# Parking half of the first MLP's input weights in the P tiles, moving their spills in the program, and loading queries first

## The chip, the cores and the metric

One core of one Trainium2 chip runs the whole kernel. The metric is the device time of one execution in microseconds (us). Each run below was taken on the same kind of core; a profile is one execution recorded by the hardware profiler.

## The reference

A Nystrom attention over 4 batches and 8 heads of 576 tokens (head size 64, 32 landmarks) is followed by two MLPs over the 2304 tokens (512 to 2048 to 512). Cut to what matters:

```python
q_lm = q.reshape(B, H, 32, 18, 64).mean(axis=3)      # landmarks of queries, and of keys alike
A, Bm, C = sm(q, k_lm), sm(q_lm, k_lm), sm(q_lm, k)  # sm: scaled scores, softmax over the last axis
Z = Bm.T / (norm1(Bm) * norminf(Bm) + 1e-6)
for _ in range(6):
    Z = 2 * Z - Z @ Bm @ Z
x = A @ Z @ C @ v                                    # then heads side by side: 2304 x 512
h = x @ w_in;  y = (h - tanh(h)) @ w_out             # first MLP
h = y @ w_in2; out = (h * tanh(softplus(h))) @ w_out2
```

## The kernel before

**Weights.** The four weight matrices come as 64-bit numbers. Each 128x512 piece (512 KB) is loaded into a *raw* buffer by the queue of SyncE (SP, line 123; there are four raw buffers). ScalarE (ACT) then makes the upper part of each float32 from it (`f32_a`, L136, called **the cast** below, into one of two *top* tiles), and VectorE (DVE) joins the lower bits to it (`f32_b`, L140, called **the join**), which frees the raw buffer. The generator `convert` runs down a list of 32 such pieces for the first MLP: 4 pieces of the input weights `w1i` (part j = 0), 9 of the output weights `w1o`, the other 12 of `w1i` (parts 1 to 3), and 7 more of `w1o`. They are numbered #1 to #32 below, in this order. It fetches three pieces ahead.

**Input weights of the first MLP.** They are folded into the attention: for each batch b and part j, `p_gen(b, j)` multiplies the little matrix `Z0` with them into a tile P (128 x 2 x 2 x 512 in float32). Batch 0 is computed in one float32 pass and uses only the first half P[:, :, 0, :]; the other batches use both halves (high and low parts). All batches need the weights, so the joined tiles of batch 0 (name `w1`, four buffers for eight tiles of 512 KB) are written out to DRAM (`w1s`, **the spill**, eight of them, issued by GpSimd's queue, POOL, in `keep_job`, L295) and read back for the later batches (`w1_load`, L617).

**Slots.** After a prologue (batch 0's attention up to `Z0`, and the first 16 casts), the first MLP runs in 128 slots, 32 per batch. Slot s multiplies one 128-wide block of P with the attention (`h1(s)`, L656 in batch 0), ACT and DVE work out h - tanh(h) (`vec(s)`: L682 s, L683 th, L685 q, L698 q on ACT; L688 mk, L694 g, L695 th, L705 g, L709 g on DVE), and `y1(s - 3)` multiplies with `w1o` (L726 in the first 16 slots). The `h` tiles have two buffers, so `h1(s)` waits for the last reader of `h1(s - 2)`, which is L695. Beside the slots run the conversion (two pieces a slot in slots 0 to 3, then one), and the attention of the next batch: its q, k and v are loaded in slot 3 (`attn_load`, L365, and `v_load`, L374 and L375), its means are DVE's L384.

**Order.** Each engine runs its instructions in the order in which a scheduler wrote them when the kernel was built; an instruction waits on its engine's queue for semaphores, and what stands behind it waits too. A DMA belongs to the queue of the engine that issues it.

Of the kernel before, what the change touches and what calls it, by code (L numbers as in the profile page):

```python
# [29 lines left out]
def kernel(  # L30
# [97 lines left out]

    tops = [const.tile([128, 512, 2], F16, name=f"top{i}") for i in range(2)]

    last_P, last_h = [None], [None]

    def f32_a(raw, i):
        top = tops[i % 2]
        with tc.issue_after(last_P[0]) if last_P[0] else ExitStack():
            A.activation(out=top[:, :, 1], in_=raw.bitcast(BF16)[:, :, 2], func=ACTF.Copy)  # L136
        return raw.bitcast(U32)[:, :, 0], top.bitcast(U32)[:, :, 0]

    def f32_b(low, top, t):
        V.scalar_tensor_tensor(out=t.bitcast(U32), in0=low, scalar=13, in1=top,  # L140
                               op0=ALU.logical_shift_right, op1=ALU.bitwise_or)
        yield 0


# [140 lines left out]
        yield 1  # L285

    def keep_job(src, g, j, a):
        def where():
            if a == 0:
                w1t[0, g, j] = w1_p.tile([128, 2, 512], F32, tag="w1", name="w1")  # L290
            return w1t[0, g, j][:, a, :]

        def done(y):
            if a == 1:
                G.dma_start(out=w1s[g, j], in_=w1t[0, g, j])  # L295
                if g:
                    ready.append(j)
        return src, done, where

    def convert(jobs, ahead=3):  # L300
        n = len(jobs)
        raws, st, halves = {}, {}, {}

        def fetch(i):
            if i < n:
                raws[i] = load_raw(jobs[i][0])

        for i in range(ahead):
            fetch(i)
# [11 lines left out]
    ready = []  # L321
    w1t = {}


# [23 lines left out]
    def heads(o, lhs, rhs):  # L348

        for c in range(4):  # L350
            ps = slice(32 * c, 32 * c + 32)
            mm(o[ps], lhs[ps], rhs[ps], start=True, stop=True, tile_position=(32 * c, 32 * c))

    ATt = {}
    adone = set()
# [3 lines left out]
    def attn_load(b, g):  # L359
        r = inp[b, g] = {}  # L360
        r["q"] = in_p.tile([128, 2, S], F32, tag="q", name="q")
        r["k"] = in_p.tile([128, 2, S + M], F32, tag="k", name="k")
        for t, src in ((r["k"], kT), (r["q"], qT)):
            if b:
                nc.sync.dma_start(out=t[:, :, 0:S], in_=src[b, 2 * g:2 * g + 2].rearrange("a p s -> p a s"))  # L365
            else:
                for a in range(2):
                    nc.sync.dma_start(out=t[:, a, 0:S], in_=src[b, 2 * g + a])
# [8 lines left out]
    def attn_pre(b):  # L377
# [17 lines left out]
            A.activation(out=(KB, QB)[x][:, g:4:2, :], in_=red[:, g, x], func=ACTF.Copy, scale=1.0 / R)  # L395

        todo = []
        for g in range(NG):
            for x, t in enumerate((ks[g], qs[g])):
                yield 1  # L400
                if todo:
                    scaled(*todo.pop())
                mean(g, x, t)
                todo.append((g, x))
                yield 1
        yield 1
        scaled(*todo.pop())
        yield 1
# [4 lines left out]
        for hf in range(2):  # L413
            for g in range(NG):
                inp[b, g]["c"] = c[:, g]
            if b == 0 and hf:
                pp = [ps_y.tile([128, 512], F32, tag="y", name="y") for g in range(NG)]
            else:
                pp = [ps_m.tile([128, 512], F32, tag="m", name="m") for g in range(NG)]
            blocks([p[:, 0:NH] for p in pp], QB, lambda ps, g, a: ks[g][ps, a, NH * hf:NH * hf + NH],  # L420
                   b > 0)
            yield 1
            n = NH - M * hf
            for g, p in enumerate(pp):
                A.activation(out=c[:, g, NH * hf:NH * hf + NH], in_=p[:, 0:NH], func=ACTF.Copy)
                V.tensor_reduce(out=mx[:, g, hf:hf + 1], in_=p[:, 0:n], axis=AX.X, op=ALU.max)
                yield 0
                if hf:
                    V.tensor_reduce(out=mx[:, g, 3:4], in_=p[:, n:NH], axis=AX.X, op=ALU.max)
                    yield 0  # L430
            yield 1
# [4 lines left out]
        V.tensor_scalar(out=nb, in0=mx[:, :, 2:4], scalar1=-0.125, scalar2=None, op0=ALU.mult)  # L436
        su = sm_p.tile([128, NG, 2], F32, tag="su", name="su", bufs=1)
        for g in range(NG):
            A.activation(out=c[:, g, S:S + M], in_=c[:, g, S:S + M], func=ACTF.Exp, bias=nb[:, g, 1:2],
                         scale=0.125, accum_out=su[:, g, 1:2])  # L440
        for g in range(NG):
            A.activation(out=c[:, g, 0:S], in_=c[:, g, 0:S], func=ACTF.Exp, bias=nb[:, g, 0:1],
                         scale=0.125, accum_out=su[:, g, 0:1])
        yield 1
        yield 1
        yield 1
# [49 lines left out]

        py = ps_m.tile([128, 512], F32, tag="m", name="m")
        for g in range(NG):
            heads(py[:, 32 * g:32 * g + 32], bb[:, 1, g, :], bb[:, 1, g, :])
        yield 1  # L500
        pv = ps_m.tile([128, 512], F32, tag="m", name="m")
        for g in range(NG):
            for j in range(5):
                n = 128 if j < 4 else 64
                for i in range(4):
                    c4 = slice(32 * i, 32 * i + 32)
                    h = 2 * (i // 2) + g
# [98 lines left out]
        adone.add((b, g, hf))  # L606
        yield 1

    Pt = {}
    done = set()  # L610

    def w1_load(n):
# [5 lines left out]

    def p_gen(b, j):
        ws = [w1t.pop((b, g, j)) for g in range(NG)]  # L620
        P = Pt[b, j] = P_p.tile([128, NG, 2, 512], F32R if b else F32, tag="P", name="P")
        pp = [ps_m.tile([128, 512], F32, tag="m", name="m") for g in range(NG)]
        blocks(pp, Z0, lambda ps, g, a: ws[g][ps, a, :])
        n = 2 * (4 * b + j) + 2
        if b or j == 3:
            w1_load(n)
            w1_load(n + 1)
        yield 1
        for g, p in list(enumerate(pp))[::1 if b else -1]:
# [382 lines left out]
    if True:  # L1012
        for g in range(NG):
            attn_load(0, g)
        setup()

        def w1i_jobs(j):
# [15 lines left out]
        while live or nc_ < PREP:  # L1033
            st = []
            if "pre" in live:
                st.append("pre")
            if n >= 15 and "pa" in live:
                st.append("pa")
            if n == 1:
                for g in range(NG):  # L1040
                    v_load(0, g)
            gens = []
            for k in st:
                if part(live[k]):
# [12 lines left out]
            n += 1  # L1057
# [103 lines left out]
```

## Time and profile before

| | |
|---|---|
| median of 3 runs | 834.3 us (833.07 to 834.39) |
| the profiled execution | 833.09 us, its span in the trace 831.3 us |
| busy: PE, DVE, ACT, POOL | 786.5, 591.7, 510.0, 207.5 us |
| DMA | 123.62 MB, busy 9 tenths or more in the first slices of the span |
| the chain that ended last | PE 62%, DVE 13%, ACT 10%, DMA 5% |

PE is TensorE's matmuls, POOL is GpSimd. A busy PE is modelled, so a stretch of 100% means that matmuls were queued without a gap. A wait in brackets behind an instruction is the idle time of its engine just before it and what ended it. Lines L... are those of the kernel before.

### The profile page before, as it was taken

What the parts mean: (1) busy time and instruction counts of PE and PEld (TensorE: products, weight loads), DVE (VectorE), ACT (ScalarE), POOL (GpSimd) and SP (SyncE); (2) the same over time, 40 slices, a digit from 0 to 9 for tenths busy, and PEclk for the clock granted to TensorE, in tenths of its full rate; (3) what the DMA queues carried; (4) which work ended last, traced back from release to release, by engine and by line L of the source; (5) the groups of instructions that cost most, each with busy time, mean ns of one, the idle gap of its engine ahead of it and who ended that gap; (6) DMA issues with size and microseconds to landing.
All of it is one profiled execution on the core that took longest, in us unless ns stands there. A gap on an engine that the chain in (4) does not pass through costs nothing.

```text
span 831.3 us, 14769 instructions
## 1 busy us (share of the span) xinstructions
PE 786.5 (95%) x5384; PEld 671.5 (81%) x5384; DVE 591.7 (71%) x1300; ACT 510.0 (61%) x1213; POOL 207.5 (25%) x233
## 2 busy tenths in 40 slices
PE   4788999999999999999998999999999999999996
PEld 1345688789987999788887888888889888888885
DVE  7679999998799877999898788786433356334332
ACT  5477877888777977787887566656223236323222
POOL 0010006786687756864340000000000000000000
PEclk9999999999999999999999999999999999999999
DMA  9899341421224100331407756864525523523402
GB/s 327 320 321 364 124 143 41 150 100 53 93 71 168 52 31 2 112 109 38 130 18 277 268 227 240 300 232 147 196 88 167 172 93 140 203 88 104 163 1 76
DMA packets 41512, 123.62 MB, mean 149 GB/s; under 512 B 5856, under 2 KB 14560, under 8 KB 38368
## 3 DMA queue, kind: packets, MB, share of 16 engines
q1 hardware_dynamic: 40288, 118.49, 40.7%
q0 software_dynamic: 1152, 4.19, 1.2%
q8 instruction: 42, 0.69, 0.3%
q14 instruction: 30, 0.25, 0.1%
HBM read 94.36 MB, written 28.31 MB: 148 GB/s over the span
## 4 chain that ended last, share of the span: by engine, by line
PE 62%; DVE 13%; ACT 10%; DMA 5%; issue 5%; POOL 5%; SPq 0%; ACTq 0%; DVEq 0%; POOLq 0%
PE h L821 6%; PE h L819 6%; PE h L820 5%; PE y L731 4%; PE y L879 4%; PE y L878 4%; PE y L877 4%; PE y L735 4%; PE y L732 4%; PE h L656 3%; PE m L334 2%; PE m L878 2%; PE m L879 2%; PE m L877 2%; DVE g L709 2%
## 5 line engine op out<-in xcount | busy, mean ns | idle before, releaser
L832 ACT ACTIVATE gg<-x 128x384 fp32r<-128x384 f32 x72 | 37.8, 525 | 167.0 <-DVE x L842 167.0
L103 POOL TENSOR_TENSOR gg<-g,gg 128x288 fp32r<-128x288 f32 x103 | 97.1, 943 | 160.7 <-ACT gg L102 158.6
L731 PE MATMUL y<-gg,w 128*128 128x288 f32 x448 | 133.9, 313 | 1.7 <-ACT raw L740 1.4
L732 PE MATMUL y<-gg,w 128*128 128x288 f32 x448 | 125.2, 295 | 0.0
L731 PEld LDWEIGHTS y<-gg,w 128*128 128x128 f32 x448 | 84.2, 188 | 21.8 <-issue 12.8
L821 PE MATMUL h<-yk,P 128*128 128x384 f32 x288 | 97.5, 339 | 3.9 <-DVE P L188 3.9
L819 PE MATMUL h<-yk,P 128*128 128x384 f32 x288 | 97.5, 338 | 2.5 <-DVE th L695 1.1
L735 PE MATMUL y<-gg,w 128*128 128x288 f32 x448 | 96.7, 297 | 2.5 <-POOL gg L103 2.5
L820 PE MATMUL h<-yk,P 128*128 128x384 f32 x288 | 96.7, 336 | 0.0
L835 DVE TENSOR_TENSOR gg<-x,gg 128x384 fp32r<-128x384 f32 x72 | 40.2, 558 | 65.9 <-ACT x L833 65.2
L732 PEld LDWEIGHTS y<-gg,w 128*128 128x128 f32 x448 | 84.4, 188 | 0.8
L688 POOL TENSOR_SCALAR mk<-s 128x288 uint8<-128x288 f32 x80 | 78.6, 982 | 10.5 <-ACT s L682 4.2
L842 DVE TENSOR_TENSOR x<-x,h 128x384 f32<-128x384 f32 x72 | 39.8, 552 | 57.8 <-PE h L821 57.8
L709 DVE COPY_PREDICATED g<-mk,th 128x288 f32<-128x288 uint8 x128 | 72.4, 566 | 5.6 <-POOL mk L688 1.7
L879 PE MATMUL y<-w,gg 128*128 128x512 f32 x192 | 75.9, 395 | 0.0
L878 PE MATMUL y<-w,gg 128*128 128x512 f32 x192 | 75.8, 395 | 0.0
L877 PE MATMUL y<-w,gg 128*128 128x512 f32 x192 | 75.3, 392 | 0.0
L735 PEld LDWEIGHTS y<-gg,w 128*128 128x128 f32 x448 | 71.3, 188 | 4.3 <-POOL gg L103 3.5
L694 DVE TENSOR_TENSOR g<-h,s 128x288 f32<-128x288 f32 x128 | 56.9, 444 | 19.4 <-ACT th L683 18.9
L698 ACT ACTIVATE q<-q,bias_c 128x288 f32<-128x288 f32 x128 | 68.6, 536 | 2.6
L682 ACT ACTIVATE s<-h 128x288 f32<-128x288 f32 x128 | 51.9, 406 | 25.2 <-PE h L660 14.9
L102 ACT ACTIVATE gg<-g 128x288 fp32r<-128x288 f32 x112 | 49.5, 442 | 23.8 <-PE y L735 11.2
(170 smaller groups left out, 1889.9 us busy)
## 6 DMA issues: line engine op xcount, KB each, us to landing
P<-w2s SPq DMA_DIRECT2D x16, 1024.0 KB, 4.8
w<-w1s SPq DMA_DIRECT2D x24, 512.0 KB, 4.5
P<-w2s SPq DMA_DIRECT2D x16, 768.0 KB, 5.8
w2s<-P SPq DMA_DIRECT2D x8, 1024.0 KB, 3.9
raw<-in_w1i_dram SPq DMA_DIRECT2D x16, 511.8 KB, 5.9
raw<-in_w1o_dram SPq DMA_DIRECT2D x16, 511.8 KB, 7.0
raw<-in_w2i_dram SPq DMA_DIRECT2D x16, 511.8 KB, 6.3
raw<-in_w2o_dram SPq DMA_DIRECT2D x16, 511.8 KB, 6.4
```

What stands on the lines that cost most here:

```text
L103: eng.tensor_tensor(out=L, in0=src, in1=f32(H), op=ALU.subtract)
L688: eng.tensor_scalar(out=mk, in0=e, scalar1=FT, scalar2=None, op0=ALU.is_ge)
L709: V.copy_predicated(out=g0, mask=mk0, data=t0)
L731: mm(yps[d], w[:, 0, c], gg[:, 0, :], start=(f == 0), stop=False)
L732: mm(yps[d], w[:, 1, c], gg[:, 0, :], start=False, stop=False)
L735: mm(yps[d], w[:, 0, c], gg[:, 1, :], start=False, stop=(f == NF - 1))
L819: mm(t, w[:, i, 0, c], y[a][:, 0], start=(a == 0), stop=False)
L820: mm(t, w[:, i, 0, c], y[a][:, 1], start=False, stop=False)
L821: mm(t, w[:, i, 1, c], y[a][:, 0], start=False, stop=(a == 1))
L877: mm(q, gg[:, 0, cs], w[:, 0, :], start=first, stop=False)
L878: mm(q, gg[:, 0, cs], w[:, 1, :], start=False, stop=False)
L879: mm(q, gg[:, 1, cs], w[:, 0, :], start=False, stop=last)
```

## The change

- `keep_job` no longer takes a `w1` buffer for the second tile of each part (g = 1): it allocates the P tile of batch 0 early and puts the weights in the half that batch 0 leaves empty, P[:, :, 1, :]. `w1` keeps the four tiles of g = 0, and none of its buffers is used twice in batch 0.
- The spills go into a list; the slot loop issues one per slot from slot 11 on (`SPILL`), on the same POOL queue. The first two `w1_load`s of batch 1 move from `p_gen(0, 3)` to slot 21.
- Batch 0's queries are loaded ahead of its keys, and its means are taken in that order. Three raw pieces, and not four, are fetched ahead of v.
- A cast is put behind batch 0's score copies and later behind its softmax exponentials on ACT (`last_act`), a join behind the score maxima on DVE (`last_mx`).
- v of batch 1 is loaded in slot 10 instead of slot 3.
- The matmuls with v (L508) are put behind those of L352.

```diff
     def f32_a(raw, i):
         top = tops[i % 2]
-        with tc.issue_after(last_P[0]) if last_P[0] else ExitStack():
+        with tc.issue_after(last_act[0]):
...
     def f32_b(low, top, t):
-        V.scalar_tensor_tensor(out=t.bitcast(U32), in0=low, scalar=13, in1=top,
-                               op0=ALU.logical_shift_right, op1=ALU.bitwise_or)
+        with tc.issue_after(last_mx[0]):
+            V.scalar_tensor_tensor(out=t.bitcast(U32), in0=low, scalar=13, in1=top,
+                                   op0=ALU.logical_shift_right, op1=ALU.bitwise_or)
...
         def where():
-            if a == 0:
+            if a == 0 and g:
+                Pt[0, j] = P_p.tile([128, NG, 2, 512], F32, tag="P", name="P")
+                w1t[0, g, j] = Pt[0, j][:, :, 1, :]
+            elif a == 0:
                 w1t[0, g, j] = w1_p.tile([128, 2, 512], F32, tag="w1", name="w1")
             return w1t[0, g, j][:, a, :]
 
         def done(y):
             if a == 1:
-                G.dma_start(out=w1s[g, j], in_=w1t[0, g, j])
+                spills.append((w1s[g, j], w1t[0, g, j]))
...
-        for g in range(NG):
-            for x, t in enumerate((ks[g], qs[g])):
-                yield 1
...
+        for g, x in ((0, 0), (0, 1), (1, 0), (1, 1)) if b else ((0, 1), (1, 1), (0, 0), (1, 0)):
+            yield 1
...
-        if b or j == 3:
+        if b:
             w1_load(n)
             w1_load(n + 1)
...
+        for x, src in (("q", qT), ("k", kT)):
+            for g in range(NG):
+                for a in range(2):
+                    nc.sync.dma_start(out=inp[0, g][x][:, a, 0:S], in_=src[0, 2 * g + a])
         setup()
...
-        cv = vec_only(convert(jobs), rate)
+        cv = vec_only(convert(jobs, {i: load_raw(jobs[i][0]) for i in range(3)}), rate)
...
-            if (nc_ < 2 + NPRE or (nc_ < PREP and "pre" not in live)):
+            if last_act[0] and (nc_ < 2 + NPRE or (nc_ < PREP and "pre" not in live)):
...
+                if i >= SPILL and spills:
+                    to, at = spills.pop(0)
+                    G.dma_start(out=to, in_=at)
+                if i == SPILL + 10:
+                    w1_load(8)
+                    w1_load(9)
...
+                    gens["a"] = attn_all(b + 1)
+                if i == (3 if b else 10):
                     for g in range(NG):
                         v_load(b + 1, g)
-                    gens["a"] = attn_all(b + 1)
```

**The order of instructions.** First place: POOL's queue from its setup to the first slot in which it computes (slot 24). Before, with the semaphores that each row waits for (DVE_49 counts DVE's instructions; w_179 and the like are `w1` tiles):

```order
L295 DMA w1s<-w_179 128x1024 [waits DVE_49]
L295 DMA w1s<-w_195 128x1024 [waits DVE_49]
L295 DMA w1s<-w_499 128x1024 [waits DVE_49]
L295 DMA w1s<-w_531 128x1024 [waits DVE_49]
L295 DMA w1s<-w_560 128x1024 [waits DVE_49]
L103 TENSOR_TENSOR gg<-g,gg 128x288 [waits DVE_49,Activation_49]
```

Of the change (the spills are L1085 there):

```order
masks.py:199 AFFINE_SELECT ident<-ident 128x128 [waits Pool_49]
L1085 DMA w1s<-w_227 128x1024 [waits DVE_49]
L1085 DMA w1s<-P 256x1x512 [waits DVE_49]
L1085 DMA w1s<-w_496 128x1024 [waits DVE_49]
L1085 DMA w1s<-w_646 128x1024 [waits DVE_49]
L104 TENSOR_TENSOR gg<-g,gg 128x288 [waits DVE_49,Activation_49]
```

In both there are eight spills in a row with nothing of POOL's between them and the setup; four of the change read P in rows of 512 numbers (2 KB) where `w1` gives rows of 1024 (4 KB). In the built program of the change the counts that they wait for are those of the joins that fill their tiles.

Second place: SP's queue from the last `w1i` piece on. Before:

```order
L123 DMA raw<-in_w1i_dram 128x2047 x12
L365 DMA k<-in_kT_dram 128x2x576
L365 DMA q<-in_qT_dram 128x2x576
L374 DMA v<-in_v_dram 128x4x256
L375 DMA v<-in_v_dram 64x256
L123 DMA raw<-in_w1o_dram 128x2047 x5
L617 DMA w_792<-w1s 128x1024
```

Of the change:

```order
L124 DMA raw<-in_w1i_dram 128x2047 x12
L370 DMA k<-in_kT_dram 128x2x576
L370 DMA q<-in_qT_dram 128x2x576
L124 DMA raw<-in_w1o_dram 128x2047 x7
L376 DMA v<-in_v_dram 128x4x256
L377 DMA v<-in_v_dram 64x256
L622 DMA w_1344<-w1s 128x1024
```

The seven `w1o` pieces #26 to #32 now stand ahead of v (k and q each come twice, v too; the second pairs are left out here).

Third place: ACT and DVE in slots 7 and 8, where the casts and joins of #26 to #28 stand (names top_127 and top_128). ACT before:

```order
L698 ACTIVATE q<-q,bias_c 128x288
L682 ACTIVATE s<-h 128x288
L395 ACTIVATE qb<-red 128x2x32
L685 ACTIVATE q<-s 128x288
L683 ACTIVATE th<-h 128x288
L393 ACTIVATE k<-red 128x2x32
L136 ACTIVATE top_128<-raw 128x512
```

ACT of the change, from the same row:

```order
L705 ACTIVATE q<-q,bias_c 128x288
L137 ACTIVATE top_128<-raw 128x512
L397 ACTIVATE qb<-red 128x2x32
L689 ACTIVATE s<-h 128x288
L690 ACTIVATE th<-h 128x288
L692 ACTIVATE q<-s 128x288
L137 ACTIVATE top_127<-raw 128x512
```

DVE before (the rows from slot 7's mk on):

```order
L688 TENSOR_SCALAR mk<-s 128x288
L694 TENSOR_TENSOR g<-h,s 128x288
L695 TENSOR_TENSOR th<-h,th 128x288
L705 TENSOR_TENSOR g<-q,g 128x288
L384 TENSOR_REDUCE red<-k 128x64
L709 COPY_PREDICATED g<-mk,th 128x288
```

DVE of the change, from the same row:

```order
L695 TENSOR_SCALAR mk<-s 128x288
L142 SCALAR_TENSOR_TENSOR w<-raw,top_128 128x512
L701 TENSOR_TENSOR g<-h,s 128x288
L702 TENSOR_TENSOR th<-h,th 128x288
L712 TENSOR_TENSOR g<-q,g 128x288
L142 SCALAR_TENSOR_TENSOR w<-raw,top_127 128x512
L716 COPY_PREDICATED g<-mk,th 128x288
L386 TENSOR_REDUCE red<-k 128x64
```

The cast and the join of #26 stand some ten rows earlier on ACT's and DVE's queues than before; those of #27 to #30 are spread over slots 7 to 10. The sequences of ACT, DVE and PE up to the join of #25 are the same in both from the start of slot 0 on; behind slot 14 a few rows of DVE and POOL trade places.

## Rows read from the trace of the kernel before

**Rows 1.** Windows: us, then busy us of each engine, PE clock, DMA share, GB/s.
```profile
60.20:85.30 25.10, 22.07 (x107) 14.41 (x105) 21.91 (x49) 18.03 (x46) 0.53 (x1) 0.93 1.02 365
85.30:130.00 44.70, 44.70 (x401) 34.11 (x400) 41.64 (x120) 36.41 (x96) 2.04 (x2) 1.00 0.32 108
```
**Rows 2.** Timeline of POOL: start us, us, instruction, idle before and its releaser.
```profile
44.29 0.53 POOL L295 DMA_DIRECT2D w1s<-w  x1 [24.25 <-DVE w L140]
...
65.48 0.53 POOL L295 DMA_DIRECT2D w1s<-w  x1 [5.59 <-DVE mk L688]
```
**Rows 3.** Timeline of SP's queue.
```profile
57.97 2.30 SPq L374 DMA_DIRECT2D v<-in_v_dram  x1
```
**Rows 4.** The second q of batch 1: duration ns, start us; issue to landing.
```profile
L365 SPq DMA_DIRECT2D q<-in_qT_dram x1: 550/550/550, 57.4 to 57.4; - x1
...
DMA to landing us min/median/max: 13.2/13.2/13.2
```
**Rows 5.** The last spill, the same way.
```profile
L295 POOL DMA_DIRECT2D w1s<-w x1: 533/533/533, 65.5 to 65.5; - x1
...
DMA to landing us min/median/max: 6.7/6.7/6.7
```
**Rows 6.** Chain of waits, 65.71: piece #26 from issue to landing.
```profile
65.71 11.10 DMA raw<-in_w1o_dram
```
**Rows 7.** Piece #29, the same way as rows 4.
```profile
L123 SPq DMA_DIRECT2D raw<-in_w1o_dram x1: 332/332/332, 70.6 to 70.6; - x1
...
DMA to landing us min/median/max: 10.0/10.0/10.0
```
**Rows 8.** Piece #4, and v right behind it, the same way.
```profile
L123 SPq DMA_DIRECT2D raw<-in_w1i_dram x1: 328/328/328, 6.9 to 6.9; - x1
...
DMA to landing us min/median/max: 8.1/8.1/8.1
...
L374 SPq DMA_DIRECT2D v<-in_v_dram x1: 379/379/379, 7.6 to 7.6; - x1
...
DMA to landing us min/median/max: 9.1/9.1/9.1
```
**Rows 9.** Timeline of ACT in slot 7 and later, columns as rows 2.
```profile
71.22 0.54 ACT L698 ACTIVATE q<-q,bias_c 128x288 f32<-128x288 f32 x1
```
**Rows 10.** Timeline of DVE, columns as rows 2.
```profile
61.34 0.69 DVE L140 SCALAR_TENSOR_TENSOR w<-raw,top 128x512 uint32<-128x512 uint32 x1 [1.19 <-ACT top L136]
...
71.00 0.30 DVE L688 TENSOR_SCALAR mk<-s 128x288 uint8<-128x288 f32 x1
...
72.31 1.34 DVE L384 TENSOR_REDUCE red<-k 128x64 f32<-128x1152 f32 x1
73.58 0.47 DVE L709 COPY_PREDICATED g<-mk,th 128x288 f32<-128x288 uint8 x1
...
77.66 0.69 DVE L140 SCALAR_TENSOR_TENSOR w<-raw,top 128x512 uint32<-128x512 uint32 x1 [1.06 <-ACT top L136]
...
80.89 0.69 DVE L140 SCALAR_TENSOR_TENSOR w<-raw,top 128x512 uint32<-128x512 uint32 x1 [0.69 <-ACT top L136]
81.50 0.45 DVE L705 TENSOR_TENSOR g<-q,g 128x288 f32<-128x288 f32 x1
...
84.97 0.45 DVE L695 TENSOR_TENSOR th<-h,th 128x288 f32<-128x288 f32 x1
```
**Rows 11.** Timeline of PE, slots 11 and 12, columns as rows 2.
```profile
82.37 1.24 PE L656 MATMUL h<-AT,P 128*128 128x288 f32 x4
...
85.48 0.75 PE L656 MATMUL h<-AT,P 128*128 128x288 f32 x2
```
**Rows 12.** Timeline of DVE in the prologue, columns as rows 2.
```profile
30.00 0.69 DVE L140 SCALAR_TENSOR_TENSOR w<-raw,top 128x512 uint32<-128x512 uint32 x1 [0.29 <-ACT top L136]
30.70 0.35 DVE L533 SCALAR_TENSOR_TENSOR yv<-yv,m 128x192 f32<-128x192 f32 x1
```
**Rows 13.** Chain of waits, 23.86: piece #9 from issue to landing.
```profile
23.86 5.25 DMA raw<-in_w1o_dram
```

More of the change, by code (lines that the diff above doesn't have):

```diff
@@ L53 @@
     PREP = 16
+    SPILL = 11
     NW = 16
@@ L298, in keep_job, with convert @@
         return src, done, where
-    def convert(jobs, ahead=3):
+    def convert(jobs, raws, ahead=3):
         n = len(jobs)
-        raws, st, halves = {}, {}, {}
+        st, halves = {}, {}
         def fetch(i):
@@ L306, in fetch @@
                 raws[i] = load_raw(jobs[i][0])
-        for i in range(ahead):
-            fetch(i)
         for i in range(n + 2):
@@ L319, in convert @@
             yield 1
-    ready = []
+    Pt = {}
+    ready, spills = [], []
     w1t = {}
@@ L351, in heads @@
             ps = slice(32 * c, 32 * c + 32)
-            mm(o[ps], lhs[ps], rhs[ps], start=True, stop=True, tile_position=(32 * c, 32 * c))
+            last = mm(o[ps], lhs[ps], rhs[ps], start=True, stop=True, tile_position=(32 * c, 32 * c))
+        return last.ins
     ATt = {}
@@ L362, in attn_load @@
         r["k"] = in_p.tile([128, 2, S + M], F32, tag="k", name="k")
[L363 to L368, printed above, removed]
+        for t, src in ((r["k"], kT), (r["q"], qT)) if b else ():
+            nc.sync.dma_start(out=t[:, :, 0:S], in_=src[b, 2 * g:2 * g + 2].rearrange("a p s -> p a s"))
     def v_load(b, g):
@@ L397, in attn_pre @@
         todo = []
-        for g in range(NG):
-            for x, t in enumerate((ks[g], qs[g])):
-                yield 1
[L401 to L405, printed above, removed]
+        for g, x in ((0, 0), (0, 1), (1, 0), (1, 1)) if b else ((0, 1), (1, 1), (0, 0), (1, 0)):
+            yield 1
+            if todo:
+                scaled(*todo.pop())
+            mean(g, x, (ks, qs)[x][g])
+            todo.append((g, x))
+            yield 1
         yield 1
@@ L424, in attn_pre @@
             for g, p in enumerate(pp):
-                A.activation(out=c[:, g, NH * hf:NH * hf + NH], in_=p[:, 0:NH], func=ACTF.Copy)
+                copied = A.activation(out=c[:, g, NH * hf:NH * hf + NH], in_=p[:, 0:NH], func=ACTF.Copy)
                 V.tensor_reduce(out=mx[:, g, hf:hf + 1], in_=p[:, 0:n], axis=AX.X, op=ALU.max)
@@ L430, in attn_pre @@
                     yield 0
+            if b == 0:
+                last_act[0] = hf and copied.ins
             yield 1
@@ L435, in attn_pre @@
         nb = sm_p.tile([128, NG, 2], F32, tag="nb", name="nb", bufs=1)
-        V.tensor_scalar(out=nb, in0=mx[:, :, 2:4], scalar1=-0.125, scalar2=None, op0=ALU.mult)
+        last_mx[0] = V.tensor_scalar(out=nb, in0=mx[:, :, 2:4], scalar1=-0.125, scalar2=None, op0=ALU.mult).ins
         su = sm_p.tile([128, NG, 2], F32, tag="su", name="su", bufs=1)
@@ L441, in attn_pre @@
         for g in range(NG):
-            A.activation(out=c[:, g, 0:S], in_=c[:, g, 0:S], func=ACTF.Exp, bias=nb[:, g, 0:1],
-                         scale=0.125, accum_out=su[:, g, 0:1])
+            last = A.activation(out=c[:, g, 0:S], in_=c[:, g, 0:S], func=ACTF.Exp, bias=nb[:, g, 0:1],
+                                scale=0.125, accum_out=su[:, g, 0:1])
+        if b == 0:
+            last_act[0] = last.ins
         yield 1
@@ L498, in attn_pre @@
         for g in range(NG):
-            heads(py[:, 32 * g:32 * g + 32], bb[:, 1, g, :], bb[:, 1, g, :])
+            last = heads(py[:, 32 * g:32 * g + 32], bb[:, 1, g, :], bb[:, 1, g, :])
         yield 1
@@ L507, in attn_pre @@
                     h = 2 * (i // 2) + g
-                    mm(pv[c4, 64 * g:64 * g + 64], cts[g][0:n, j, c4],
-                       inp[b, i % 2]["v"][0:n, j, 64 * h:64 * h + 64],
-                       start=(j == 0), stop=(j == 4), tile_position=(0, 32 * i))
+                    with tc.issue_after(last):
+                        mm(pv[c4, 64 * g:64 * g + 64], cts[g][0:n, j, c4],
+                           inp[b, i % 2]["v"][0:n, j, 64 * h:64 * h + 64],
+                           start=(j == 0), stop=(j == 4), tile_position=(0, 32 * i))
         yield 1
@@ L620, in p_gen @@
         ws = [w1t.pop((b, g, j)) for g in range(NG)]
-        P = Pt[b, j] = P_p.tile([128, NG, 2, 512], F32R if b else F32, tag="P", name="P")
+        if b:
+            Pt[b, j] = P_p.tile([128, NG, 2, 512], F32R, tag="P", name="P")
+        P = Pt[b, j]
         pp = [ps_m.tile([128, 512], F32, tag="m", name="m") for g in range(NG)]
@@ L624, in p_gen @@
         n = 2 * (4 * b + j) + 2
-        if b or j == 3:
+        if b:
             w1_load(n)
@@ L631, in p_gen @@
                 with tc.high_priority(60):
-                    last_P[0] = A.activation(out=P[:, g, 0, :], in_=p, func=ACTF.Copy).ins
+                    last_act[0] = A.activation(out=P[:, g, 0, :], in_=p, func=ACTF.Copy).ins
                 done.add((b, g, j))
```

3 lines of the change are left out of this document (1 added, 2 removed).

## The prediction

> **What bounds the kernel now.** I read the windows first, to cut the span by what limits it. From 85.3 us on PE has no gap (44.70 us busy of 44.70 up to 130 us, [rows 1]); the 25 us before that are different: DMA engines at their full share, DVE busy 21.9 of 25.1 us, PE 22.1. The change moves loads, casts and spills, all of them work of the first 85 us, so its worth is how much earlier PE gets into its gapless stretch. That is a question of two places: the prologue up to slot 0, and slots 5 to 12.
>
> Next the timelines of PE and DVE there. `h1` of slots 11 and 12 starts at 82.37 and 85.48 [rows 11], each behind an L695 of DVE (84.97 and 0.45 us later PE goes, [rows 10]). So DVE is the clock of slots 4 to 12, and what can be won is DVE's idle time. It has three sizeable gaps there, all before a join that waits for its cast: 1.19 us before the join of #24, 1.06 before #26, 0.69 before #28 [rows 10]; together 2.94. Last the landings tell why. Pieces come in the order in which SP issued them: #26 was issued at 65.71 and landed 11.10 us later, at 76.81 [rows 6]; #29 was issued at 70.6 and landed at 80.6 [rows 7]. Three pieces in 3.8 us are **1.27 us a piece**: this is a queue that is drained at its full rate, so a piece lands when all that stands ahead of it has landed.
>
> **The spills.** If slot 11 held them back, six spills of 512 KB would leave the stream between 44 and 72 us. But the order of POOL shows nothing that holds them: the eight DMAs stand right behind the setup, and each waits for DVE alone, for the join that fills its tile. Before, the third spill went off at 44.29 after an idle time of 24.25 us that a join ended, and the last at 65.48 in the same way [rows 2]. A position in the program is no position in time on a queue that is empty in front of it. So I forecast that spills 3 to 8 start where they start now, and I cost their move at **0**. It is a gain only if something else holds POOL, and I see nothing that could.
>
> Four spills now read P in 2 KB rows. The nearest rows: 512 KB of v in 1 KB rows landed at 7.6 + 9.1 = 16.7, 1.7 us behind piece #4 at 6.9 + 8.1 = 15.0 [rows 8], against 1.27 for a piece in 4 KB rows. So a spill in 2 KB rows costs the stream between 0 and 0.43 us more. Three such spills (the fourth, sixth and eighth) come ahead of #26: 0 to 1.3 us; I take 0, since the rows are nearer to a piece's in number than v's are to them, and keep 1.3 for the range. The Trainium skill says in "Perfetto Trace Analysis", section DMA Optimizations, that transfers under 2 KB carry a large overhead and that going from 2 KB to 4 or 8 KB can improve throughput much. By that rule the spills would have become dearer and #26 later, the upper end of my bound; by the row, at most that.
>
> **v behind the w1o pieces.** On SP, v of batch 1 stood ahead of #26; its first issue alone held the queue for 2.30 us [rows 3], and v's 1.1 MB were drained ahead of #26. Now #26 comes right behind the second q, which lands at 57.4 + 13.2 = 70.6 [rows 4]. One piece later is 71.8. The last spill, issued at 65.5, lands at 72.2 [rows 5] and shares the stream, which costs up to 1.27: I take **72.5** for #26, with 71.8 and 73.8 (72.5 and 1.3 for the 2 KB rows) as ends. So #26 lands 4.3 us earlier, and #27 to #29 follow at 1.27 each. v is now late next: it goes off when the join of #28 has freed a buffer, about 78 us, and it is read only after 100 us, so this hides.
>
> **But it is also needed earlier.** The schedule puts the cast of #26 behind slot 7's second Square on ACT (71.22 and 0.54 long, so from 71.8, [rows 9]) and its join right behind slot 7's mk on DVE (71.00, [rows 10]). Before, both stood behind slot 9's Exp and the last mean, where DVE came at 76.6. The need moves up by 5.1 us, more than the landing. ACT stands at the cast until 72.5, and behind it wait qb, and s, th and q of slot 8; DVE stands at the join until 73.3 (a cast takes 0.8), and behind it the g, th and g of slot 7. DVE was free at 71.2: a new wait of **2.1 us**.
>
> **The sum up to slot 12.** DVE from slot 7's mk (71.00) to slot 10's th, start to start by [rows 10]: mk, g, th, g take 1.31 (71.00 to 72.31), a mean 1.27 (to 73.58), a select 0.37 (its 0.47 less what it overlaps), a join 0.61 (80.89 to 81.50). Of the change there are three slots (3.93), mk and g of slot 10 (0.6), two means (2.54), three selects (1.1) and five joins (3.05): 11.2. With 2.1 for #26, and 0.2 for #27 (its cast stands behind qb, s, th and q of slot 8, 1.1 us on ACT), th of slot 10 comes at 71.0 + 13.5 = 84.5, against 84.97 now: **0.4 us earlier**, with ends of 1.1 earlier and 0.9 later by the landing of #26. The waits before the joins of #26 and #28 have not gone, they have moved to slot 7. The gap before #24 stays: its landing depends on spills that have not moved.
>
> **The prologue.** Queries first lets the score matmuls with the first half start before the last mean, and with the casts behind the copies the maxima are done about 0.6 us earlier. But the joins of #2 to #4, now behind the softmax, free their raw buffers some 4 us later, so #6 to #8 are asked for later while DMA runs dry for about a us. What ends the prologue is the Newton steps (L533), and the fifth stands at 30.70 behind the join of #9, which waited 0.29 for its cast [rows 12] and that for a landing 5.25 us after 23.86 [rows 13]. By my count #9 is issued about a us later with less queue ahead of it, and lands at 29.1 again. I take **0**; the ends are 0.6 earlier (then the join's 0.61 leaves the path, and the steps are back to back) and 0.6 later.
>
> Everything else is cost nothing: the later `w1_load`s land by about 91 us and are needed after 120; behind slot 14 some rows of DVE and POOL trade places beside a PE with no gap, worth up to 1 us either way, which I keep for the range.
>
> So 833.09 - 0.4 + 0 = 832.7 for the profiled execution's own time; that execution lies 1.2 below the median of the runs shown, so in their terms **833.9 us**.
>
> **Rivals.**
> 1. *The spills do go later.* Then the stream up to #26 is about 7 us shorter, all three gaps close, and 2.9 us are won: 831.0. Against it stands the order of POOL. Chance 0.08.
> 2. *The early ends add up*: #26 at 71.8 (1.1), the prologue (0.6) and some of the us behind slot 14: 1.8 to 2.5 us, 832 or a little less. For it: the landing of #26 is known to a us only. Chance 0.16.
> 3. *Slower: the early cast stands in front of a later piece.* ACT and DVE both queue behind #26, so each us by which it lands later is lost whole. It decides from a landing at 74.6 on (72.5, the 0.4, and 1.7 of margin). Landing as now, at 76.81, it would cost 76.81 - 72.5 - 0.4 = 3.9 us: 838. For it: 2 KB rows, and a q that lands behind dearer spills. Against it: v no longer stands ahead. Chance 0.16.
>
> **How the numbers follow.** 0.2% is 1.7 us, about what a measurement of this kernel can tell from no change. My forecast, within that, has 0.60; rivals 1 and 2 end on the faster side (0.24), rival 3 on the slower (0.16). The range takes in the whole of rival 1 and the first half of rival 3: 830.6 to 836.5.
>
> **What would show it.** In the profile of the changed kernel: eight POOL DMAs at about 20, 23, 44, 48, 52, 56, 59 and 65 us (spills at 90 to 120 us would prove me wrong on the first step); #26 landing near 72.5; a wait of about 2 us before DVE's first join behind 71 us, with ACT's cast waiting for a raw piece; the gap before the join of #24 still there; `h1` of slot 12 near 85.1, and slot 0 near 36.4. A slot 12 before 83 or behind 87 would make the prediction wrong.

## The result, and the profile after

The changed kernel is **slower**: 838.18 us (median of 4 runs, 837.46 to 839.56) against 833.97 us of the kernel before beside it, a ratio of 1.0054 with a 95% interval of 1.0036 to 1.0071. I had forecast 833.9 us, no change, and the result lies outside the range of 830.6 to 836.5.

| | before | after |
|---|---|---|
| the profiled execution; its span | 833.09; 831.3 us | 837.46; 835.7 us |
| first `h1` of slot 0 | 36.43 | 39.74 |
| `h1` of slot 12 | 85.48 | 87.95 |
| piece #9: issued, landed | 23.86, 29.11 | 25.02, 32.52 |
| piece #26: issued, landed | 65.71, 76.81 | 60.99, 75.58 |

POOL's timeline of the changed kernel answers to [rows 2] (columns as there):

```profile
20.28 0.77 POOL L1085 DMA_DIRECT2D w1s<-w  x1 [18.98 <-DVE red L487]
23.45 0.70 POOL L1085 DMA_DIRECT2D w1s<-P  x1 [2.40 <-DVE n L522]
48.16 0.56 POOL L1085 DMA_DIRECT2D w1s<-w  x1 [24.02 <-DVE w L142]
...
68.37 0.68 POOL L1085 DMA_DIRECT2D w1s<-P  x1 [4.29 <-DVE mk L695]
```

The eight spills go off at 20.28 to 68.37, each behind its join: the list and the slot number have moved nothing in time. Where another row of DVE is named (red, n, mk), it is one that ran just behind the join of the tile's second piece.

The first loss is in the prologue. Its windows (columns as in rows 1):

```profile
14.00:18.00 4.00, 1.14 (x6) 1.14 (x7) 3.93 (x14) 2.72 (x10) 0.00 (x0) 0.62 1.09 323
18.00:22.00 4.00, 3.53 (x82) 2.44 (x84) 3.41 (x13) 4.00 (x10) 0.77 (x1) 0.50 0.52 170
22.00:30.00 8.00, 3.53 (x80) 2.07 (x70) 5.72 (x20) 2.68 (x5) 0.70 (x1) 0.50 0.95 333
```

From 18 to 22 us the DMA engines are half idle: a share of 0.52 and 170 GB/s, where the kernel before had 1.02 and 387 in the same stretch:

```profile
18.00:22.00 4.00, 3.61 (x72) 2.36 (x74) 3.95 (x16) 3.11 (x8) 0.55 (x1) 1.00 1.02 387
```

Then the timeline of DVE, joins (L142) and Newton steps (L539) alone:

```profile
15.10 0.68 DVE L142 SCALAR_TENSOR_TENSOR w<-raw,top 128x512 uint32<-128x512 uint32 x1
...
19.28 0.69 DVE L142 SCALAR_TENSOR_TENSOR w<-raw,top 128x512 uint32<-128x512 uint32 x1 [0.22 <-ACT top L137]
...
24.35 0.65 DVE L142 SCALAR_TENSOR_TENSOR w<-raw,top 128x512 uint32<-128x512 uint32 x1
24.92 0.34 DVE L539 SCALAR_TENSOR_TENSOR yv<-yv,m 128x192 f32<-128x192 f32 x1
...
26.15 0.69 DVE L142 SCALAR_TENSOR_TENSOR w<-raw,top 128x512 uint32<-128x512 uint32 x1 [0.27 <-ACT top L137]
26.76 0.35 DVE L539 SCALAR_TENSOR_TENSOR yv<-yv,m 128x192 f32<-128x192 f32 x1
...
29.47 0.69 DVE L142 SCALAR_TENSOR_TENSOR w<-raw,top 128x512 uint32<-128x512 uint32 x1 [1.98 <-ACT top L137]
30.08 0.35 DVE L539 SCALAR_TENSOR_TENSOR yv<-yv,m 128x192 f32<-128x192 f32 x1
31.65 0.69 DVE L142 SCALAR_TENSOR_TENSOR w<-raw,top 128x512 uint32<-128x512 uint32 x1 [1.23 <-ACT top L137]
32.26 0.35 DVE L539 SCALAR_TENSOR_TENSOR yv<-yv,m 128x192 f32<-128x192 f32 x1
33.41 0.69 DVE L142 SCALAR_TENSOR_TENSOR w<-raw,top 128x512 uint32<-128x512 uint32 x1 [0.80 <-ACT top L137]
34.02 0.35 DVE L539 SCALAR_TENSOR_TENSOR yv<-yv,m 128x192 f32<-128x192 f32 x1
```

Join #1 is the first row, #2 comes at 19.28 (before: 14.69), #5 at 24.35 and #9 at 33.41; #3 and #4, which write into P, are left out. Three joins between the steps wait 1.98, 1.23 and 0.80 us for their casts. The fifth step, 30.70 before [rows 12], comes at 34.02. SP's row of piece #9, as [rows 13] before:

```profile
L124 SPq DMA_DIRECT2D raw<-in_w1o_dram x1: 328/328/328, 25.0 to 25.0; - x1
...
DMA to landing us min/median/max: 7.5/7.5/7.5
```

It landed 7.5 us after its issue, not 5.25, and slot 0 follows on PE:

```profile
39.74 1.81 PE L663 MATMUL h<-AT,P 128*128 128x288 f32 x3 [1.23 <-ACT P L639]
```

The second place, slots 7 and 8, answers to [rows 9] and [rows 10]: ACT's cast of #26, and DVE's joins of #23, #24 and #26.

```profile
75.61 0.78 ACT L137 ACTIVATE top<-raw 128x512 f16<-128x512 bf16 x1 [2.62 <-DMA raw<-in_w1o_dram]
```

```profile
62.53 0.69 DVE L142 SCALAR_TENSOR_TENSOR w<-raw,top 128x512 uint32<-128x512 uint32 x1 [1.26 <-ACT top L137]
...
64.23 0.68 DVE L142 SCALAR_TENSOR_TENSOR P<-raw,top 128x512 uint32<-128x512 uint32 x1
...
76.41 0.69 DVE L142 SCALAR_TENSOR_TENSOR w<-raw,top 128x512 uint32<-128x512 uint32 x1 [2.23 <-ACT top L137]
```

The new wait is there, 2.23 us long, at a landing of 75.58 and not 72.5. The gap of 1.19 us before #24 has moved to #23 (1.26).

The third place is behind slot 14. POOL and PE in slot 31:

```profile
148.39 0.81 POOL L104 TENSOR_TENSOR AT<-c,AT 128x288 fp32r<-128x288 f32 x1 [2.31 <-ACT AT L103]
149.15 0.82 POOL L104 TENSOR_TENSOR gg<-g,gg 128x288 fp32r<-128x288 f32 x1
```

```profile
150.03 0.53 PE L742 MATMUL y<-gg,w 128*128 128x288 f32 x2 [0.54 <-POOL gg L104]
...
151.88 0.99 PE L663 MATMUL h<-AT,P 128*128 128x288 f32 x3 [0.53 <-DVE th L702]
```

An attention row of POOL (AT) stands ahead of gg and waits 2.31 us for ACT; PE's matmul with gg then waits 0.54, and the `h1` of slot 31 another 0.53 for th. Before, that `h1` waited 0.18:

```profile
147.77 1.24 PE L656 MATMUL h<-AT,P 128*128 128x288 f32 x4 [0.18 <-DVE th L695]
```

The clearest view of where it was lost is the start of one DVE row in each slot, the select (L709 before, L716 after), against the kernel before. In the table below each number is after less before in us, read from the profiled executions; "end" is the span.

| kernel | slot 0 | slot 12 | slot 16 | slot 31 | end |
|---|---|---|---|---|---|
| the change | +3.32 | +2.08 | +2.16 | +3.99 | +4.34 |
| E1 casts free | +0.12 | -0.18 | +0.04 | +1.86 | +2.69 |
| E2 behind only | +2.20 | +2.56 | +2.56 | +2.55 | +2.86 |
| E3 parked only | -0.73 | -0.98 | -0.97 | -0.97 | +0.16 |
| E4 spills held | +1.81 | -2.98 | -3.04 | -1.20 | -0.84 |
| E5 held, casts free | -0.81 | -5.62 | -5.69 | -3.86 | -3.25 |
| E6 v in slot 3 | +3.98 | +4.43 | +5.04 | +5.04 | +5.24 |
| E7 as E5, v in slot 3 | -0.82 | -1.95 | -0.64 | -0.61 | +0.62 |
| E9 #4 in AT | +2.05 | -0.54 | -0.48 | +1.34 | +2.29 |
| E10 as E5, #4 in AT | -0.46 | -5.55 | -5.61 | -3.77 | -2.48 |
| E11 as E5, v in slot 4 | -0.59 | -5.45 | -4.74 | -3.65 | -1.17 |
| E12 queries first only | -0.70 | -0.79 | -0.80 | -0.77 | -0.42 |
| E13 one cast ahead | +3.35 | +2.82 | +2.87 | +4.67 | +5.28 |

By this row the change lost 3.3 us up to slot 0, won 1.2 by slot 12, and lost 1.8 between slots 16 and 31; the rest of the span adds 0.35. But the row is DVE's, and PE need not have done the same work when it starts. PE's matmuls of `y1` up to slot 16's select, before and after:

```profile
L726 PE MATMUL y<-g,w x116: 406/406/847, 42.3 to 106.0; 128*128 128x288 f32 x116
```

```profile
L733 PE MATMUL y<-g,w x112: 406/406/510, 46.4 to 105.2; 128*128 128x288 f32 x112
```

At slot 16 the changed kernel has four of them still to do, at 0.24 us from one to the next: 0.97 us. The same four are put off in E1, E4, E5, E9, E10 and E13, and in no other run. Counted in PE's work, these seven kernels stand 0.97 us worse at slot 16 than the table shows, and the change won 0.2 us from slot 0 to slot 16 and lost 0.9 behind it. PE's order thus differs from that of the kernel before already from slot 8 on, and not only DVE's and POOL's behind slot 14.

The last column is the loosest: from slot 31 to the end the kernels differ by up to 2.5 us among themselves with the same work. E5 and E11 show one place of it, in the second MLP, where PE waited for DVE's x 0.2 us in all in E5 and 2.0 in E11.

### The profile page after: what moved, and what is told of

It is laid out like the page before. It is cut to its first block, busy times and chain, and to the rows that moved or that the text cites. A ratio compares the mean times of both kernels' runs of the same rounds, so it can differ in the third digit from the quotient of the medians.

```text
span 835.7 us, 14768 instructions
## 1 busy us (share of the span) xinstructions
PE 783.0 (94%) x5384; PEld 670.8 (80%) x5384; DVE 594.0 (71%) x1300; ACT 509.9 (61%) x1213; POOL 208.1 (25%) x233
## 3 DMA queue, kind: packets, MB, share of 16 engines
q0 software_dynamic: 1152, 4.19, 1.3%
## 4 chain that ended last, share of the span: by engine, by line
PE 63%; DVE 13%; ACT 9%; DMA 6%; issue 5%; POOL 4%; SPq 0%; DVEq 0%; ACTq 0%; POOLq 0%
PE h L828 6%; PE h L826 6%; PE h L827 6%; PE y L886 5%; PE y L885 5%; PE y L884 5%; PE y L738 4%; PE y L742 3%; PE y L739 3%; DMA raw<-in_w1o_dram 3%; PE m L885 2%; PE m L886 2%; PE m L884 2%; DVE g L716 2%; PE h L663 2%
## 5 line engine op out<-in xcount | busy, mean ns | idle before, releaser
L716 DVE COPY_PREDICATED g<-mk,th 128x288 f32<-128x288 uint8 x128 | 74.5, 582 | 5.0 <-POOL mk L695 0.9
L137 ACT ACTIVATE top<-raw 128x512 f16<-128x512 bf16 x64 | 50.0, 785 | 24.7 <-DMA raw<-in_w1o_dram 8.4
```

What stands on the lines that cost most here:

```text
L716: V.copy_predicated(out=g0, mask=mk0, data=t0)
```

## The experiments

Theory 1, formed from the trace above: casts and joins behind the softmax give the raw buffers back late, DMA runs dry, and what it didn't bring stands in front of the later pieces; the Newton steps then wait for the joins. Theory 2: the rows that trade places behind slot 14 cost 1.8 us, and v's slot decides them. The rivals were TensorE's clock, the spills in 2 KB rows, and the place of the joins as such.

**E1: casts and joins free.**

```diff
-        with tc.issue_after(last_act[0]):
+        with tc.issue_after(last_P[0]) if last_P[0] else ExitStack():
...
-        with tc.issue_after(last_mx[0]):
...
-            if last_act[0] and (nc_ < 2 + NPRE or (nc_ < PREP and "pre" not in live)):
+            if (nc_ < 2 + NPRE or (nc_ < PREP and "pre" not in live)):
```

> The changed kernel, but casts and joins are again ordered as before the change: a cast only behind the last P eviction, a join behind nothing. Theory 1 (joins #2 to #4 behind the softmax free their raw buffers late, so DMA runs dry at 18 to 22 us and the Newton steps wait for the joins of #7 to #9): slot 0 back at 36.4 to 37, DMA share about 1 at 18 to 22 us, time 834.5 to 835.5, that is 838.2 less the 3.3 of the prologue. Rival (the two prologue spills, one of them in 2 KB rows, or the lower TensorE clock cost the prologue): slot 0 stays at 39 to 40 and the time at 837.5 to 838.5.

Measured: 835.64 us, ratio 1.0017 (1.0006 to 1.0028), just above the expected 835.5. Slot 0 is back at 36.54. The windows and piece #9:

```profile
18.00:36.00 18.00, 12.54 (x220) 6.76 (x218) 12.11 (x38) 9.04 (x19) 0.70 (x1) 0.50 0.96 345
```

```profile
DMA to landing us min/median/max: 5.3/5.3/5.3
```

This also rules out the clock as the cause of the loss. The granted clock in 18 to 36 us is 0.50 (1.2 GHz) here as in the changed kernel, and slot 0 is 3.2 us earlier. The run keeps the parking, the queries first and the matmuls with v behind those of L352, so these cost nothing at slot 0 where casts and joins are free. What is left of the loss shows in the table behind slot 16 (+1.86 at slot 31).

**E2: casts behind the scores, alone,** in the kernel before; three pieces are fetched ahead as in the change.

```diff
-        with tc.issue_after(last_P[0]) if last_P[0] else ExitStack():
+        with tc.issue_after(last_act[0]):
...
+        with tc.issue_after(last_mx[0]):
...
+            if last_act[0] and (nc_ < 2 + NPRE or (nc_ < PREP and "pre" not in live)):
```

> The kernel before with one part of the change alone: casts behind the score copies and the softmax, joins behind the maxima. Theory 1: slot 0 at 39 to 40, DMA share near 0.5 at 18 to 22 us, time 836 to 838. Rival: slot 0 at 36 to 37 and 833.5 to 834.5.

Measured: 836.73 us, 1.0033 (1.0022 to 1.0043), as expected; slot 0 at 38.62, a little before the expected 39, and the 2.2 to 2.6 us stay to the end.

```profile
18.00:36.00 18.00, 11.52 (x213) 7.07 (x219) 12.67 (x40) 9.82 (x21) 1.32 (x2) 1.00 0.88 313
```

The 1.00 for the clock in this row is not a reading: PE's matmuls run at the low level here too (last section). One part alone gives over half of what the whole change costs, as Theory 1 has it; which part beside it adds the other 1.1 us at slot 0 was not tried.

**E13: one cast ahead of the exponentials.**

```diff
-        if b == 0:
-            last_act[0] = last.ins
```

> The changed kernel without the second half of the ordering on ACT: casts stand behind the score copies, but not behind the exponentials. In the written order this puts one cast (that of #2) ahead of the exponentials and moves the cast of #3 one place up. Theory 1 (each join that is late holds its raw buffer, and each piece behind it is asked for late): join #2 at 16 to 16.8 instead of 19.28, #6 issued at about 17 instead of 20.00, slot 0 at 38.2 to 39.0, that is 0.7 to 1.5 earlier, as with one more raw buffer; time 836.5 to 837.5. Rival (the place of the joins between the Newton steps costs): slot 0 at 39.5 to 39.8, time 838.

Measured: 838.04 us, 1.0050 (1.0033 to 1.0066), and slot 0 at 39.78: the rival's numbers. #6 was asked for at 17.78, as Theory 1 expected, and it didn't help. Piece #9 shows why:

```profile
L124 SPq DMA_DIRECT2D raw<-in_w1o_dram x1: 328/328/328, 26.4 to 26.4; - x1
...
DMA to landing us min/median/max: 6.2/6.2/6.2
```

It was issued at 26.40, behind the join of #5, which frees its buffer, and landed at 32.56, where it landed in the changed kernel too. So it is not "each late join", but those up to #5 and what stands in the queue, and they act through #9. Over all the runs this reads:

| kernel | #9 landed | slot 0 | difference |
|---|---|---|---|
| E3 | 28.23 | 35.68 | 7.45 |
| E12 | 28.51 | 35.73 | 7.22 |
| before | 29.11 | 36.43 | 7.32 |
| E1 | 29.19 | 36.54 | 7.35 |
| E4 | 31.01 | 38.24 | 7.23 |
| E9 | 31.26 | 38.48 | 7.22 |
| E2 | 31.40 | 38.62 | 7.22 |
| the change | 32.52 | 39.74 | 7.22 |
| E13 | 32.56 | 39.78 | 7.22 |
| E6 | 33.13 | 40.40 | 7.27 |
| E11, E5, E7, E10 | 27.23, 27.18, 27.05, 26.61 | 35.84, 35.62, 35.60, 35.97 | 8.4 to 9.4 |

Slot 0 starts 7.2 to 7.5 us behind the landing of #9 wherever that is later than 28. In the last four kernels #9 is there in time and the Newton steps run back to back. In E13 the maxima were also done late (nb at 16.43, 15.06 in the changed kernel), so the run can't show alone what one cast is worth; that place of the joins costs by itself is ruled out by the table, not by this run.

**E9: one more raw buffer, casts and joins where the change has them.** Piece #4 goes into an AT tile that is idle until slot 0, and four pieces are fetched ahead instead of three.

```diff
-    def load_raw(src, pool=None):
+    def load_raw(src, spare=False):
+        if spare:
+            raw = AT_p.tile([128, NG, 2, HS], F32, tag="AT", name="raw")...
...
-    def convert(jobs, raws, ahead=3):
+    def convert(jobs, raws, ahead=4):
```

> The changed kernel with one more raw buffer: piece #4 waits in an AT tile that is idle until slot 0, so each later piece can be asked for one join earlier. Casts and joins keep their places. Theory 1 (the raw buffers, held longer, starve the stream): DMA share at 18 to 22 us above 0.8, #9 lands at 30.5 to 31.5 instead of 32.52, slot 0 at 37.5 to 38.7, time 836 to 837. Rival (the joins between the Newton steps cost by their place alone): slot 0 stays at 39.5 to 39.8, time 838.

Measured: 835.51 us, 1.0013 (1.0004 to 1.0022), a little faster than expected. Slot 0 came at 38.48 and #9 landed at 31.26, both as expected; the DMA share from 18 to 22 us, 0.69, stayed below the expected 0.8:

```profile
18.00:22.00 4.00, 3.53 (x58) 2.75 (x58) 3.35 (x12) 3.54 (x10) 0.62 (x1) 0.50 0.69 275
```

The dry stretch has 275 GB/s instead of 170, and slot 0 comes 1.26 us earlier. Another 1.3 are won by slot 12, where four pieces ahead put #26 before k and q of batch 1 (it lands at 65.95), which the expectation had left out.

**E3: parking alone,** in the kernel before.

```diff
-            if a == 0:
+            if a == 0 and g:
+                Pt[0, j] = P_p.tile([128, NG, 2, 512], F32, tag="P", name="P")
+                w1t[0, g, j] = Pt[0, j][:, :, 1, :]
+            elif a == 0:
```

> The kernel before with one part of the change alone: the weights of g = 1 wait in the empty half of P, the spills stay where they are in the program. Theory 1: same as before, 833.5 to 834.5, slot 0 at 36.4, POOL's DMAs at the times of before. Rival (spills in 2 KB rows are what costs): 835 to 837, with later landings behind each P spill.

Measured: 834.70 us, 1.0008 (0.9995 to 1.0022): no change that can be told. Its spills from P take what those from `w1` took: from issue to landing 7.65, 7.74, 7.85 and 6.89 us for the second, fourth, sixth and eighth, against 8.20, 7.61, 7.63 and 6.67 before, the same 7.53 on the mean. So 2 KB rows cost nothing that can be told, the lower end of my bound.

**E12: queries first, alone,** in the kernel before.

```diff
+        for x, src in (("q", qT), ("k", kT)):
+            for g in range(NG):
+                for a in range(2):
+                    nc.sync.dma_start(out=inp[0, g][x][:, a, 0:S], in_=src[0, 2 * g + a])
```

> The kernel before with one part of the change alone: batch 0's queries loaded ahead of its keys and its means in that order. The prediction's 0 to 0.6 earlier maxima: nb at 14.7 to 15.3, slot 0 at 35.9 to 36.5, time 833.3 to 834.3. Rival (this part belongs to the loss): slot 0 at 37 or later, 835 or more.

Measured: 834.21 us, 0.9998 (0.9984 to 1.0012), no change, with nb at 15.04 and slot 0 at 35.73.

**E6: v in slot 3 again.**

```diff
-                if i == (3 if b else 10):
+                if i == 3:
```

> The changed kernel with v of batch 1 loaded in slot 3 again. In the written order this takes away the differences of POOL and PE behind slot 14. Theory 2 (these rows cost the 1.9 us that the changed kernel loses between slots 16 and 30): the offset to before stays as it is at slot 12 (about 2 to 2.5 us), and the time is 836.0 to 836.8. Rival (the loss behind slot 14 comes from the later reads of the weights or from the spills): 838, with the offset still growing to about 4.

Measured: 838.31 us, 1.0043 (1.0029 to 1.0056): no gain, and the rival's 838. The mechanism behind slot 16 is as Theory 2 has it, not the rival's: the offset is +5.04 at slot 16 and +5.04 at slot 31, and PE's order is that of the kernel before again. But #26 lands at 80.82 behind v, and slots 0 to 12 lose what the order gives back. In the table every kernel with v in slot 10 loses 1.8 us from slot 16 to slot 31 (the change, E1, E4, E5, E9, E10, E13), every one with v in slot 3 nothing (E2, E3, E6, E7, E12), and slot 4 (E11) 1.1. Of the 1.8 us, 0.97 are the `y1` matmuls put off ahead of slot 16.

**E4: spills really held.** One tiny copy ties POOL's queue to slot 10.

```diff
+                if i == SPILL:
+                    hold = sm_p.tile([128, 8], F32, tag="hold", name="hold", bufs=1)
+                    held[0] = G.tensor_copy(out=hold, in_=sv[s - 1][2][:, 0:8]).ins
                 if i >= SPILL and spills:
                     to, at = spills.pop(0)
-                    G.dma_start(out=to, in_=at)
+                    with tc.issue_after(held[0]):
+                        G.dma_start(out=to, in_=at)
```

> The changed kernel, with one tiny POOL copy of slot 10's q ahead of the eight spills, so that they really go off from slot 11 on (at about 88 us). If the spills cost what a piece costs in the stream, #26 lands some 5 us earlier, the prologue is 1 to 2 us shorter (spills 1 and 2 no longer beside #6 to #9), and the time is 834 to 836. If the loss of the change is latency and DMA that runs dry alone, slot 0 stays near 39.5, slots 3 to 9 gain at most 1.5, and the time is 837 to 838.

Measured: 831.87 us, 0.9972 (0.9962 to 0.9982), **faster than the kernel before**, and better than either number expected.

```profile
79.99 0.19 POOL L1085 COPY hold<-q 128x8 f32<-128x8 f32 x1 [78.69 <-ACT q L705]
80.23 0.78 POOL L1089 DMA_DIRECT2D w1s<-w  x1
```

The first spill leaves at 80.23, #26 lands at 70.14, and slots 0 to 12 win 4.8 us (+1.81 to -2.98).

**E5: held, and casts free** (the diffs of E4 and E1 together).

> The changed kernel with the spills really held to slot 11 and casts and joins free in the prologue. If the two repairs add up (6.3 us of the held spills, 2.5 of the free casts): 829 to 830, slot 0 near 36. If they repair the same late landings: 830.5 to 831.9.

Measured: 830.40 us, 0.9955 (0.9939 to 0.9970), between the two expectations. At slot 12 the gains of E1 and E4 add up (-5.62); of the sum of their times, 829.3, 1.1 us are missing.

```profile
28.55 0.35 DVE L539 SCALAR_TENSOR_TENSOR yv<-yv,m 128x192 f32<-128x192 f32 x1 [0.38 <-PE m L357]
...
29.89 0.35 DVE L539 SCALAR_TENSOR_TENSOR yv<-yv,m 128x192 f32<-128x192 f32 x1 [0.38 <-PE m L357]
```

Between the Newton steps DVE now waits for PE alone. Three variations of E5 follow.

**E7: v in slot 3** (E6's diff in E5, which its text calls the run before).

> The kernel of the run before in this call, with v of batch 1 in slot 3 as well. If the order behind slot 14 costs 1.9 us by itself: 1.5 to 2 us less than that run. Rival: v stands ahead of #26 again and costs slots 7 to 10 what the order gives back: the same time.

831.80 us, 0.9972 (0.9959 to 0.9984): no gain over E5, so the rival and not Theory 2's sum. The order behind slot 16 is repaired (-0.64 to -0.61), but slot 12 stands at -1.95 and not -5.62.

**E10: #4 in the AT tile** (E9's diff in E5).

> Spills held and casts free, and piece #4 in the idle AT tile as well (one raw buffer more). If raw buffers still starve the stream there: slot 0 below 35.3 and 829.5 or less. Theory 1 (with casts free the raw buffers come back in time, and the Newton steps set slot 0): slot 0 at 35.4 to 35.8, time 830 to 831.

831.03 us, 0.9957 (0.9944 to 0.9971), slot 0 at 35.97, a little behind the expected 35.8: nothing is left for a buffer to win.

**E11: v in slot 4.**

```diff
-                if i == (3 if b else 10):
+                if i == (3 if b else 4):
```

> Spills held and casts free, v of batch 1 loaded in slot 4: on SP it stands behind #26 and #27, and the written order of POOL behind slot 14 is that of before. Theory 2: the offset to before stays flat from slot 14 on, and the time is 828.5 to 829.6. Rival: #28 to #32 land behind v, some 4 us later, slots 9 to 12 wait for them, and the time is 830.5 to 832.

830.53 us, 0.9949 (0.9935 to 0.9963): the rival's time, the same as E5 within what can be told. The offset does not stay flat, it grows by 1.1 us from slot 16 to slot 31. At slot 16 the two stand alike once E5's four `y1` matmuls are counted (-4.74 here, -5.69 + 0.97 = -4.72 there): slot 4 gives nothing back.

## Why the prediction was wrong

**The step that failed is the prologue**, the term that I set to 0 with ends of 0.6: it measured +3.3 us. I had seen that "the joins of #2 to #4, now behind the softmax, free their raw buffers some 4 us later, so #6 to #8 asked for later while DMA runs dry for about a us", and I had the issue of #9 right: 1.16 us later. What was wrong is "with less queue ahead of it, and lands at 29.1 again": #9 would have had to take 4.1 us instead of 5.25 [rows 13], and it took 7.5. There was more ahead of it, not less. When it was issued, three pieces were still to land (#6 to #8, at 25.26, 28.59 and 30.77); before, two were (#7 and #8, at 24.18 and 27.86). Here the dry stretch didn't shorten the queue, it put off what was behind it. It was also longer than "about a us": from 18 to 22 us the stream moved 217 GB/s less than before, 0.87 MB or 1.7 pieces; at 1.27 us a piece that is 2.1 of the 3.4 us by which #9 landed later. The rest is not placed row by row; DMA moved less than before in 22 to 30 us too (333 against 355 GB/s).

**Step 1, the spills, was right.** A place in the program is none on an empty queue: they went off at 20 to 68 us. E4 shows the other half of it: with a data dependence in front they do wait, and that is worth 6.3 us against the change and 2.0 against before. Rival 1 had this mechanism, but at 2.9 us; between slots 0 and 12 E5 wins 4.5 us more than E1 does, with #19 landing at 47.19 instead of 49.22 and #26 at 67.16 instead of 72.83.

**2 KB rows** cost nothing that can be told (E3), and the trace shows no smaller transfers. POOL's queue has 1152 packets and 4.19 MB before and after; a packet for each 2 KB row would have made 512 more. The rule of the Trainium skill ("Perfetto Trace Analysis", section DMA Optimizations) that transfers under 2 KB carry a large overhead, and that going from 2 KB to 4 or 8 KB can improve throughput much, is thus not put to the test by any run here.

**v behind the w1o pieces, and the early cast: right for DVE, and measured by E1**, whose slot 0 is that of before. #26 landed at 72.83 (72.5 forecast), DVE waited 3.03 us before its join (2.1 forecast), and th of slot 10 came at 84.61, 0.36 earlier than before (0.4 forecast). But I had taken DVE for the clock of these slots, and at slot 12 PE no longer waited for it: `h1` came at 86.15, straight behind `y1` matmuls, 0.67 later than before and within the ends that I gave. PE's rows in E1:

```profile
75.14 2.29 PE L663 MATMUL h<-AT,P 128*128 128x288 f32 x4 [3.01 <-DVE th L702]
77.22 4.11 PE L733 MATMUL y<-g,w 128*128 128x288 f32 x14
...
85.18 1.13 PE L733 MATMUL y<-g,w 128*128 128x288 f32 x4
86.15 1.13 PE L663 MATMUL h<-AT,P 128*128 128x288 f32 x4
```

PE had lost time at slot 9: it waited 3.01 us for th, and TensorE's granted clock was at 0.50 from 74.91 to 78.32 us, so that the four matmuls of `h1` took 2.29 us and not 1.13. In the changed kernel it waited 2.21 us there, and they took 1.24. Counted in PE's work, E1 lost 0.9 us from slot 0 to slot 16 (+0.12, and 0.04 + 0.97), and the changed kernel won 0.2; how much of the difference is the clock's and how much the shorter wait's was not tried. DVE's wait before #26 is shorter there too (2.23 us against 3.03); that slots which start later wait less for loads is argued, not tried by itself.

**Behind slot 14** I kept 1 us either way for the range and 0 for the sum. By the select it measured 1.8 in every kernel with v in slot 10. Of that, 0.97 are the four `y1` matmuls that the order had put off to behind slot 16; the other 0.9 are PE's waits for gg and th in the rows above (0.54 + 0.53, against 0.18 before). So the loss there is 0.9 us, within the 1 us that I kept.

**Rival 3** gave 838 us and the right sign, by a mechanism that wasn't the cause: #26 landed past its point of decision (75.58 against 74.6) because the slots and their joins were later by then, not because of dearer spills.

Left open: the differences after slot 31, and why TensorE's clock rose at different times ahead of the softmax (last section).

## What to carry to other kernels

Where loads share a few buffers, the instruction that frees a buffer is on the load's path: moving it behind other work can cost the time in which DMA runs dry, at the next place that waits for a piece: here that was the join of #9. A row of one engine can come earlier without the kernel gaining: count also what the engine that bounds the kernel has done by then. Moving an instruction in the program defers it only if its queue has something in front of it or its data depends on the later moment; to hold a DMA back, give its queue an instruction that reads the late data. And a change of a load's slot can reorder what has nothing to do with it: compare the written order of all engines to the end, and price it.

## What the runs showed of the hardware

TensorE's clock. In the changed kernel the granted clock was at 1.00 (2.4 GHz) from 11.54 to 14.96 us and at 0.50 (1.2 GHz) from there to 45.68; PE stood idle for 4.00 us up to 16.86, at the transposes of L458. In the traces of the kernel before and of E2 the clock's record begins only at 40.83 and 43.65 us, and a window ahead of that reads 1.00 without one. Their matmuls show the low level there. The kernel before:

```profile
23.72 0.86 PE L352 MATMUL m<-yv 32*32 32x96 f32 x16 [0.43 <-ACT yv L520]
36.43 2.29 PE L656 MATMUL h<-AT,P 128*128 128x288 f32 x4 [1.23 <-ACT P L632]
...
73.65 1.13 PE L656 MATMUL h<-AT,P 128*128 128x288 f32 x4
...
109.69 0.53 PE L352 MATMUL m<-yv 32*32 32x96 f32 x16
```

Four matmuls of `h1` take 2.29 us in slot 0 and 1.13 in slot 9, and the sixteen of a Newton step 0.86 us in the prologue and 0.53 in batch 1. In E2 slot 0 takes 2.29 us as well, and the sixteen take 0.86 in the prologues of the changed kernel, E1, E2 and E3 alike. So from 18 us to slot 0 these kernels ran at the same level; what it costs there is open, since no run has these steps at the full one.

Ahead of the softmax the level did differ. In the changed kernel the last score matmuls took 0.42 us each, at full level, and ended at 12.86; the maxima were done at 15.06 (nb). In E4, E6, E9 and E13 they took 0.71 and ended at 14.16 to 14.74, the record of the full level begins at 13.71 to 15.21, and the maxima were done at 16.16 to 16.61. So slot 0 of these four compares with that of the changed kernel to no better than about 1.5 us; in E4 and E9 it came earlier in spite of that.
